# Denominators by block transposes, fewer transfers and a replanned order in an attention and gated-MLP kernel

## The chip, the cores and the metric

The kernel runs on one core of one Trainium2 chip. A core has five engines that run their own instruction streams in order: TensorE (matmul, "PE"), VectorE ("DVE"), ScalarE ("ACT"), GpSimd ("POOL") and SyncE ("SP"), which here issues nearly all transfers between memory (DRAM) and the on-chip buffer. The transfers themselves run on 16 DMA engines. Matmul results go to PSUM, which has eight banks; the kernel uses three as a shared pool (`bs`), two for the large products (`bz`) and three for the outputs (`po`). The metric is device time in microseconds, the median of several runs.

## The reference

Four batches, four heads, 1088 positions, head dimension 32. First a linear attention with a quadratic feature map, whose output x (1088 x 128 per batch) feeds a gated MLP that mixes over positions with a 1088 x 1088 weight matrix.

```python
phi(x) = outer(S1 @ x, S2 @ x)                 # 8 x 8 = 64 features per head and position
kv  = einsum('bhsf,bhsd->bhfd', phi(k), v)
z   = sum(phi(k), over positions)
num = einsum('bhsf,bhfd->bhsd', phi(q), kv)
den = einsum('bhsf,bhf->bhs', phi(q), z) + 1e-06
x   = num / den                                # heads side by side: 128 columns

h    = gelu_tanh(x @ w_in)                     # 1024 columns
u, v = h[..., :512], h[..., 512:]
v_n  = layernorm(v) * g_ln
v_s  = einsum('ts,bsd->btd', w_sg, v_n) + b_sg
out  = x + (u * v_s) @ w_out
```

## The kernel before

Everything is float32; the accurate products are made of three matmuls on a high and a low part (`_h`, `_l`). Columns of positions are cut in three chunks of 362 or 364 (`CH`, `CA`), and the 512 gate columns in four blocks of 128.

The first 50 us are the head: batch 0's attention, the first loads and splits, ordered by a table (`HEAD`). All behind it is built as a list of tasks with an engine, an estimated duration, what they read and write, and buffers they take and free (`Plan.add`). `Plan.order` (L113) then simulates the engines: at each step it issues the task that can begin first, and among equals the one with the earliest due time. Due times come from the TensorE tasks, sorted by `pos`, and are carried back through the dependencies. The result is a fixed order of instructions on each engine.

For each later batch `attention(b)` (L1000) makes x. It loads k and v, makes the key features (L1014 to L1028: `bs`, `kb`, `kp`) and kv with its two parts (`kvh`, `kvl`). Then, for each of three chunks of positions: load q (`qld`, L1039), two parts, project (L1045 to L1047) to 64 rows, copy to `ab` (L1050), store to DRAM as `dq` (L1051), and load back spread out into four tiles e0 to e3 of 128 rows. Of these, two are broadcasts of one transfer each (L1053), and two are written by `spread` (L790 to L793) in eight transfers of 16 rows each. VectorE multiplies them (L1060), ScalarE and VectorE make the two parts (L1061 into `r`, L1062 into `e`), TensorE multiplies by kv (L1069 to L1071). ScalarE copies the result into two tiles: r2 holds the denominators, each repeated over the 32 rows of its head, and r3 the numerators (L1075, L1076).

The denominators then go through DRAM (`dd`): one row of each head out (L1079), back packed into at most 112 rows of 13 (L1080), epsilon and reciprocal (L1081), out (L1082), and back as a broadcast over 32 rows (L1083) into r4. VectorE multiplies r3 by r4 (L1084), and `x_h` and `x_l` are written (L1086, L1087).

From x come the gate's v columns (L1101 to L1103), gelu and its sums (L1110, L1113), the norm (L296 to L332) and the normalised v in `vn` (L340).

`pair(b, p, ...)` (L1130) makes two 128-column blocks of the position mixing with fewer products than plain blocks would take: it uses sums and differences of blocks of the weights. These combinations are made once by `combine` (L961) in eight rounds: load two pieces of the raw weights into `tmp` (L973), combine and split them on VectorE and ScalarE (L978 to L988), store to the DRAM tensors `td` (L991; in the trace `t`, and `tb` for the saved original, L963). Since they don't fit on chip, `stream` (L994) loads the current combination over columns 362 to 723 of `w_h` and `w_l` between products (L996), 24 times in all, four times a pair of transfers. `unit` makes u, `evac` and `gate` bring a product out of PSUM and multiply (`gt`, `gh`, `gl`: L859, L872 to L874), and `gate` ends in the output matmuls (L881 to L883); `store` adds x and stores the output.

In the planner's costs a transfer on SP takes its size over 330 KB per us, at least 0.08 us; `spread` with its eight issues is one task of 200 KB, and a transfer is done 2.0 us after that. `SIDE` gives, per batch, a first due time and a step for the attention's matmuls; output matmuls are due `DELAY` behind their place in the main order.

Of the kernel before, what the change touches and what calls it, by code (L numbers as in the profile page):

```python
# [9 lines left out]
F32 = mybir.dt.float32  # L10
# [24 lines left out]
DELAY = 5.83  # L35
SIDE = [
    dict(k=(0, 0.0241), q=(0.065, 0.0107), n=(0.0314, 0.1822), v=(0.6703, 0.0732)),
    dict(k=(0.0669, 0.0251), q=(0, 0.0934), n=(0.0321, 0.1642), v=(0.3581, 0.0424)),
    dict(k=(0.1528, 0.0085), q=(0, 0.142), n=(0, 0.2213), v=(0.4732, 0.0276)),
]  # L40
START = dict(PE=51.0, V=50.5, A=49.5, G=42.0, SP=22.0)
# [37 lines left out]
class Plan:  # L79
# [9 lines left out]
    def add(self, eng, dur, f, r=(), w=(), take=(), free=(), pos=None, late=None, start=None, after=()):  # L89
# [15 lines left out]
        late = self.LATE.get(eng, 0) if late is None else late  # L105
        self.tasks.append(dict(eng=eng, dur=dur, f=f, deps=deps, take=take, free=list(free), pos=pos, late=late, start=start))
# [6 lines left out]
    def order(self, free, t0):  # L113
# [21 lines left out]
        clock = dict(free)  # L135
        can = {e: [] for e in clock}

# [8 lines left out]
        def enter(i):  # L146
            if T[i]["eng"] is None:
                done(i, T[i]["start"])
            else:
                can[T[i]["eng"]].append(i)  # L150

# [3 lines left out]
        while len(seq) < sum(t["eng"] is not None for t in T):  # L155
            best = None
            for e, c in can.items():
                for i in c:
                    x = max(clock[e], ready[i])
                    for k in T[i]["take"].values():  # L160
                        if not units[k]:
                            break
                        x = max(x, min(units[k])[0])
                    else:
                        key = (x, last[i], i)
                        if best is None or key < best[0]:
                            best = key, i, e
            if best is None:
                raise RuntimeError("stuck: " + str([(T[i]["take"], i) for c in can.values() for i in c][:20]) + str({k: [g for g in self.got if cls[g] == k][-8:] for k in units}))
            (x, _, _), i, e = best  # L170
# [20 lines left out]
def tile_kernel(ctx: ExitStack, tc: tile.TileContext, qd, kd, vd, sd, wd, bd, wind, gd, woutd, identd, outd):  # L191
# [60 lines left out]
    rt, et = ([swap.tile([P, 3 * P], F32, tag=f"{x}{i}", name=f"{x}{i}") for i in range(n)] for x, n in (("r", 5), ("e", 4)))  # L252
# [7 lines left out]
    drt = [const([P, 13], f"dr{i}") for i in range(2)]  # L260
# [504 lines left out]
    t4a = []  # L765
# [586 lines left out]
```

## Time and profile before

| | us |
|---|---|
| median of 3 runs | 434.6 |
| lowest and highest | 433.58, 434.79 |
| the profiled execution | 435.59 |
| its span, first to last instruction | 433.8 |
| its mean granted TensorE clock | 0.921 |

The profile is of one execution. A row of the timeline gives the start, the duration, the engine, the line, the operation with output and inputs, and in brackets the idle time before it and what ended that. SPq is SP's queue of issues. In the chain, which follows the work that ended last backwards, "DMA a<-b" is a transfer from its issue to its landing. A group's row ends in its busy time, the mean duration in ns and the idle time before it. Windows give busy time per engine in a stretch, with the granted clock (1.00 is full speed).

### The profile page before, as it was taken

To read this page: it belongs to the slowest core of one execution; us is meant where nothing else is said; L and a number is where in the kernel's file an instruction comes from. 1 tells how busy PE (TensorE), PEld (TensorE's weight loads), DVE (VectorE), ACT (ScalarE), POOL (GpSimd) and SP (SyncE) were. 2 spreads that over 40 slices of the span, in tenths; PEclk is the share of its full clock that TensorE was granted. 3 is DMA by queue.
4 is the path that set the end of the run, shared out by engine and by line. 5 is a ranking of instruction groups with operands and counts; after the bars stand their busy time and mean duration, and the time that the engine had idled before them with its cause. 6 is when DMAs were issued, how large, how long until landed. Compare 5 with 4: busy or idle time off the path is not lost.

```text
span 433.8 us, 6285 instructions
## 1 busy us (share of the span) xinstructions
PE 365.0 (84%) x1952; PEld 335.1 (77%) x1952; DVE 265.2 (61%) x619; ACT 216.4 (50%) x517; POOL 22.7 (5%) x85
## 2 busy tenths in 40 slices
PE   8989968939487687786968997996876999999996
PEld 7866668939486567686857997996765899899995
DVE  5788957825654483783663545883635565877553
ACT  4667622613234694661363796442422878544320
POOL 0010000000000050000000112000000022100000
PEclk9999997979699998896958999899698899999999
DMA  8990034634476473567663894065844584296351
GB/s 270 402 322 20 0 75 135 178 90 109 112 165 190 102 233 103 165 178 224 161 190 89 240 324 139 13 200 136 231 108 120 155 275 137 71 306 227 103 172 51
DMA packets 63077, 70.72 MB, mean 163 GB/s; under 512 B 10720, under 2 KB 60356, under 8 KB 63044
## 3 DMA queue, kind: packets, MB, share of 16 engines
q1 hardware_dynamic: 62900, 70.24, 54.8%
q8 instruction: 15, 0.25, 0.2%
q14 instruction: 18, 0.15, 0.1%
q10 hardware_dynamic: 144, 0.09, 0.1%
HBM read 61.20 MB, written 9.10 MB: 162 GB/s over the span
## 4 chain that ended last, share of the span: by engine, by line
PE 31%; DMA 24%; SPq 16%; DVE 12%; ACT 9%; issue 5%; POOL 3%; DVEq 0%; POOLq 0%; ACTq 0%
SPq L792 12%; DMA r<-dd 7%; PE bz L927 5%; PE bz L929 5%; PE bz L928 5%; DMA tmp<-in_w 4%; DMA dq<-ab 3%; DMA dd<-dr 3%; ACT vn L340 2%; DMA w_h<-t 2%; ACT kp L1113 2%; PE pz L725 2%; PE pab L601 2%; ACT vn L1110 2%; SPq L1053 1%
## 5 line engine op out<-in xcount | busy, mean ns | idle before, releaser
L927 PE MATMUL bz<-w_h,ar 128*128 128x362 f32 (+1 forms) x288 | 100.5, 349 | 6.0 <-DMA w_h<-t 3.8
L928 PE MATMUL bz<-w_h,ar 128*128 128x362 f32 (+1 forms) x288 | 98.8, 343 | 0.4 <-DVE ar L905 0.4
L929 PE MATMUL bz<-w_l,ar 128*128 128x362 f32 (+1 forms) x288 | 98.8, 343 | 0.0
L927 PEld LDWEIGHTS bz<-w_h,ar 128*128 128x128 f32 x288 | 58.4, 203 | 8.0 <-DMA w_h<-t 4.3
L928 PEld LDWEIGHTS bz<-w_h,ar 128*128 128x128 f32 x288 | 58.0, 201 | 1.4 <-DVE ar L905 0.6
L929 PEld LDWEIGHTS bz<-w_l,ar 128*128 128x128 f32 x288 | 57.6, 200 | 0.2 <-DMA w_l<-t 0.2
L1060 DVE TENSOR_TENSOR e<-e,e 128x364 f32<-128x364 f32 (+1 forms) x18 | 9.6, 536 | 45.6 <-DMA e<-dq 38.4
L1061 ACT CAST r<-e 128x364 fp32r<-128x364 f32 (+1 forms) x18 | 8.9, 494 | 55.0 <-DVE e L1060 54.9
L874 DVE TENSOR_TENSOR gl<-gt,gh 128x362 fp32r<-128x362 f32 (+1 forms) x47 | 25.1, 533 | 17.3 <-ACT gh L873 17.2
L873 ACT CAST gh<-gt 128x362 fp32r<-128x362 f32 (+1 forms) x47 | 23.2, 493 | 23.9 <-DVE gt L872 22.9
L340 ACT ACTIVATE vn<-vn,st 128x512 f32<-128x512 f32 x36 | 27.9, 811 | 9.9 <-POOL st L332 5.8
L904 ACT CAST ar<-vn 128x512 fp32r<-128x512 f32 x40 | 24.7, 617 | 13.3 <-PE bz L929 12.9
L905 DVE TENSOR_TENSOR ar<-vn,ar 128x512 fp32r<-128x512 f32 x40 | 27.4, 684 | 3.8 <-ACT ar L904 3.4
L849 ACT ACTIVATE u<-bs 128x362 f32<-128x362 f32 (+1 forms) x48 | 22.3, 468 | 12.8 <-PE bs L845 11.4
L883 PE MATMUL po<-gl,wout_h 128*128 128x362 f32 (+1 forms) x47 | 16.7, 354 | 12.7 <-DVE gl L874 12.7
L872 DVE TENSOR_TENSOR gt<-gt,u 128x362 f32<-128x362 f32 (+1 forms) x47 | 25.0, 532 | 1.5 <-ACT u L849 0.9
L859 DVE SCALAR_TENSOR_TENSOR gt<-bz,g_col,b_bc 128x362 f32<-128x362 f32 (+1 forms) x31 | 18.3, 591 | 9.3 <-PE bz L939 5.1
L1101 PE MATMUL bs<-win_h,x_h 128*128 128x512 f32 x27 | 12.7, 471 | 11.2 <-ACT x_h L1086 4.8
L843 PE MATMUL bs<-x_h,win_h 128*128 128x362 f32 (+1 forms) x48 | 16.6, 345 | 6.5 <-ACT r L1076 3.8
L1084 DVE TENSOR_TENSOR r<-r,r 128x364 f32<-128x364 f32 (+1 forms) x9 | 4.8, 537 | 26.9 <-DMA r<-dd 26.9
L883 PEld LDWEIGHTS po<-gl,wout_h 128*128 128x128 f32 x47 | 9.3, 199 | 13.7 <-DVE gl L874 13.6
L1022 PE MATMUL bs<-vx,kp 128*128 128x128 f32 x108 | 19.1, 310 | 0.8 <-DVE kp L268 0.8
(267 smaller groups left out, 803.2 us busy)
## 6 DMA issues: line engine op xcount, KB each, us to landing
w_h<-t SPq DMA_DIRECT2D x72, 181.0 KB
w_l<-t SPq DMA_DIRECT2D x72, 181.0 KB
w_f<-in_w SPq DMA_DIRECT2D x9, 544.0 KB
t<-tmp SPq DMA_DIRECT2D x48, 90.5 KB
w_h<-tb SPq DMA_DIRECT2D x24, 181.0 KB
w_l<-tb SPq DMA_DIRECT2D x24, 181.0 KB
tmp<-in_w SPq DMA_DIRECT2D x16, 181.0 KB
vx<-in_v SPq DMA_DIRECT2D x8, 288.0 KB
```

Source lines behind the costliest of these rows:

```text
L340: A.activation(self.vn(t), self.vn(t), AF.Identity, bias=self.nm[:, t : t + 1], scale=self.rs[:, t : t + 1])
L792: last = load(e[16 * i : 16 * i + 16], d)
L849: add("A", 0.05 + ac(cw), lambda: A.activation(utt[plan.got[u]][:, :cw], ps(k)[:, :cw], AF.Gelu_apprx_tanh), r=[k], take={u: "u"}, free=[k])
L872: add("V", dv(cw), lambda: V.tensor_mul(gt(k)[:, :cw], gt(k)[:, :cw], utt[plan.got[u]][:, :cw]), r=[u], w=[k], free=[u])
L873: add("A", ac(cw), lambda: A.copy(ght[plan.got[h]][:, :cw], gt(k)[:, :cw]), r=[k], take={h: "gh"})
L874: add("V", dv(cw), lambda: V.tensor_sub(glt[plan.got[l]][:, :cw], gt(k)[:, :cw], f32(ght[plan.got[h]][:, :cw])), r=[h, k], take={l: "gl"}, ...
L883: mm(o, lhsT=wout_h[:, db], rhs=hl, start=False, stop=i == NB, skip_group_check=True)
L904: add("A", ac(n), lambda: A.copy(dst[:, 0], q()), r=r, w=[key])
L905: add("V", dv(n), lambda: V.tensor_sub(dst[:, 1], q(), f32(dst[:, 0])), r=r, w=[key])
L927: mm(o, lhsT=ar[e][:, 0, t], rhs=wh, start=first, stop=False, skip_group_check=True)
L928: mm(o, lhsT=ar[e][:, 1, t], rhs=wh, start=False, stop=False, skip_group_check=True)
L929: mm(o, lhsT=ar[e][:, 0, t], rhs=wl, start=False, stop=last, skip_group_check=True)
```

## The change

It has three parts.

The denominators stay on chip. r2 holds each denominator on all 32 rows of its head, so a transpose of its 32 x 32 blocks on VectorE leaves in every 32nd column of r4 the denominators of 32 positions, one in each row. Epsilon and reciprocal act on 12 columns; ScalarE spreads each over 32 columns of r2, and a second transpose brings them to the layout of the numerators. The columns of r2 behind the shortest chunk are set to one once.

Transfers are merged. The four spread tiles become two tiles of two halves, ea and eb; each half of eb is loaded by one transfer whose source repeats 16 rows eight times, and product, cast and subtraction act on both halves at once. `combine` stores three combinations' parts by three transfers instead of six, and the saved original by five instead of eight. `stream` loads two slices of `w_h` by one transfer; `w_l` stays at one each. The keys of the dependencies are kept apart for the two parts.

The planner counts 0.47 us of SP for each issue (1.0 for the two of ea or eb), and a transfer's end by a ring that moves 300 KB per us. `SIDE` becomes a table with a due time for each attention matmul group, `UNITS` and `OUTS` give offsets of the unit and output matmuls, and `STARTS` the batches' starts. The search for the next task is also rewritten, with the same rule.

```diff
-DELAY = 5.83
+START = dict(PE=51.0, V=50.5, A=49.5, G=42.0, SP=22.0)
+STARTS = (0.0, 96.0, 166.0, 236.0)
 SIDE = [
-    dict(k=(0, 0.0241), q=(0.065, 0.0107), n=(0.0314, 0.1822), v=(0.6703, 0.0732)),
-    dict(k=(0.0669, 0.0251), q=(0, 0.0934), n=(0.0321, 0.1642), v=(0.3581, 0.0424)),
...
+        k=[-69.5, -129.7, -258.62, 75.49, -16.81, -86.04, 99.22, -240.4, 467.74],
+        m=[44.69, -2.17, -319.74, 128.68, -11.47, -380.37, -268.7, -327.69, -223.35],
+        q=[-500.43, 26.57, 6.61],
+        n=[-114.19, -31.31, 54.44, 107.92, 21.3, 18.55],
+        v=[79.56, 57.62, 53.21, 95.41, 35.99, 315.99, 135.47, 134.1, 132.66],
...
+UNITS = [
+    [-875.2, 12.55, 557.21],
...
+OUTS = [
+    [12.14, 10.35, 36.95],
...
-        late = self.LATE.get(eng, 0) if late is None else late
+        late = (2.3 + kb / 300 if eng == "SP" else self.LATE.get(eng, 0)) if late is None else late
...
+            if e == "SP":
+                ring = max(ring, clock[e]) + T[i]["kb"] / 300
+                T[i]["late"] = max(2.1, ring + 1.7 - clock[e])
...
-    dma = lambda kb: max(0.08, kb / 330.0)
+
+    def load_(_, kb, f, **kw):
+        return add("SP", 0.47, f, kb=kb, **kw)
...
     def combine():
+        load_("td", 740, lambda: load(td[3, :, 0].rearrange(by), f32(w_h[:, 4:8, 362:724])), r=[("w", t + 4, 1, 0) for t in range(4)], w=[("td", "b", t, 0) for t in range(4)])
         for t in range(4):
-            add("SP", dma(370), lambda t=t: [load(td["b"][t, 0], f32(w_h[:, t + 4, 362:724])), load(td["b"][t, 1], f32(w_l[t + 4][:, 362:724]))],
-                r=[("w", t + 4, 1)], w=[("td", "b", t)])
...
-                for n, i, j in (("1", 0, 0), ("3", 1, 1), ("2", 3, 2)):
-                    add("SP", dma(186), lambda t=t, c=c, s=s, hi=hi, n=n, i=i, j=j: [
-                        load(td[n][t, 0][:, c : c + HW], f32(hi[:, j])), load(td[n][t, 1][:, c : c + HW], s[:, i])],
-                        r=[k[i], hk[j]], w=[("td", n, t)])
+                nk = [("td", n, t, i) for i in range(2) for n in "132"]
+                load_("td", 278, lambda t=t, c=c, hi=hi: load(td[:3, t, 0, :, c : c + HW].rearrange(by), f32(hi)), r=hk, w=nk[:3])
+                load_("td", 186, lambda t=t, c=c, s=s: load(td[:2, t, 1, :, c : c + HW].rearrange(by), s[:, :2]), r=k[:2], w=nk[3:5])
+                load_("td", 93, lambda t=t, c=c, s=s: load(td[2, t, 1, :, c : c + HW], s[:, 3]), r=[k[3]], w=nk[5:])
 
     def stream(n, half):
         for t in range(4):
-            add("SP", dma(370), lambda t=t: [load(f32(w_h[:, t + half, 362:724]), td[n][t, 0]), load(f32(w_l[t + half][:, 362:724]), td[n][t, 1])],
-                r=[("td", n, t)], w=[("w", t + half, 1)])
+            if t % 2 == 0:
+                load_("w", 371, lambda t=t: load(f32(w_h[:, half + t : half + t + 2, 362:724]), TD[n][t : t + 2, 0].rearrange(by)),
+                    r=[("td", n, x, 0) for x in (t, t + 1)], w=[("w", half + x, 1, 0) for x in (t, t + 1)])
+            load_("w", 186, lambda t=t: load(f32(w_l[half + t][:, 362:724]), TD[n][t, 1]), r=[("td", n, t, 1)], w=[("w", half + t, 1, 1)])
...
-            add("SP", dma(93), lambda cw=cw, ci=ci: load(dq[ci][:, :cw], abt[:, :cw]), r=["ab"], w=[("dq", ci)])
-            for p in range(2):
-                add("SP", dma(200), lambda cw=cw, ci=ci, p=p: load(
-                    here(f"e{p}")[:, :cw], dq[ci][16 * p : 16 * p + 16, :cw].unsqueeze(1).broadcast_to([16, R, cw])),
-                    r=[("dq", ci)], w=[("e", p)])
-                add("SP", dma(200), lambda cw=cw, ci=ci, p=p: spread(
-                    here(f"e{2 + p}")[:, :cw], dq[ci][32 + 16 * p : 48 + 16 * p, :cw]),
-                    r=[("dq", ci)], w=[("e", 2 + p)])
-            for p in range(2):
-                add("V", dv(cw), lambda p=p, cw=cw: V.tensor_mul(now[f"e{p}"][:, :cw], now[f"e{p}"][:, :cw], now[f"e{2 + p}"][:, :cw]), r=[("e", 2 + p)], w=[("e", p)])
-                add("A", ac(cw), lambda p=p, cw=cw: A.copy(here(f"r{p}", F32R)[:, :cw], now[f"e{p}"][:, :cw]), r=[("e", p)], w=[("r", p)])
-                add("V", dv(cw), lambda p=p, cw=cw: V.tensor_sub(here(f"e{2 + p}", F32R)[:, :cw], now[f"e{p}"][:, :cw], f32(now[f"r{p}"][:, :cw])), r=[("e", p), ("r", p)], w=[("e", 2 + p)])
+            load_("", 93, lambda cw=cw, ci=ci: load(dq[ci][:, :cw], abt[:, :cw]), r=["ab"], w=[("dq", ci)])
+            for i, e in enumerate(("ea", "eb")):
+                def fill(cw=cw, ci=ci, i=i, e=e):
+                    d = dq[ci][32 * i : 32 * i + 32, :cw].rearrange("(p x) c -> x p c", p=2)
+                    o = here(e)[:, :, :cw]
+                    if i:
+                        for p in range(2):
+                            load(o[:, p], dq[ci][32 + 16 * p : 48 + 16 * p, :cw].unsqueeze(0).broadcast_to([R, 16, cw]))
+                    else:
+                        for p in range(2):
+                            load(o[:, p], dq[ci][16 * p : 16 * p + 16, :cw].unsqueeze(1).broadcast_to([16, R, cw]))
+
+                add("SP", 1.0, fill, kb=373, r=[("dq", ci)], w=[e])
+            add("V", dv(2 * cw), lambda cw=cw: V.tensor_mul(now["ea"][:, :, :cw], now["ea"][:, :, :cw], now["eb"][:, :, :cw]), r=["eb"], w=["ea"])
+            add("A", ac(2 * cw), lambda cw=cw: A.copy(here("r0", F32R)[:, :, :cw], now["ea"][:, :, :cw]), r=["ea"], w=["r0"])
+            add("V", dv(2 * cw), lambda cw=cw: V.tensor_sub(here("eb", F32R)[:, :, :cw], now["ea"][:, :, :cw], f32(now["r0"][:, :, :cw])), r=["ea", "r0"], w=["eb"])
...
-            n = CD[ci]
-            dr = drt[0][: H * (cw // n), :n]
-            add("SP", 0.08, lambda cw=cw, ci=ci: load(dd[ci][0, :, :cw], now["r2"][0:P:32, :cw]), r=[("r", 2, 0), ("r", 2, 1)], w=[("dd", ci)])
-            add("SP", 0.08, lambda cw=cw, ci=ci, n=n, dr=dr: load(dr, dd[ci][0, :, :cw].rearrange("h (i n) -> h i n", n=n)), r=[("dd", ci)], w=["dr"])
-            add("V", 0.5, lambda dr=dr: [V.tensor_scalar(dr, dr, EPS, None, op0=ALU.add), V.reciprocal(dr, dr)], w=["dr"])
-            add("SP", 0.08, lambda cw=cw, ci=ci, n=n, dr=dr: load(dd[ci][1, :, :cw].rearrange("h (i n) -> h i n", n=n), dr), r=["dr"], w=[("dd", ci)])
-            add("SP", dma(190), lambda cw=cw, ci=ci: load(now["r4"][:, :cw], dd[ci][1, :, :cw].unsqueeze(1).broadcast_to([H, 32, cw])), r=[("dd", ci)], w=[("r", 4)])
-            add("V", dv(cw), lambda cw=cw: V.tensor_mul(now["r3"][:, :cw], now["r3"][:, :cw], now["r4"][:, :cw]), r=[("r", 4)], w=[("r", 3, 0), ("r", 3, 1)])
+            add("V", dv(3 * P), lambda: V.transpose(now["r4"], now["r2"]), r=[("r", 2, 0), ("r", 2, 1)], w=["r4"])
+
+            def invert():
+                V.tensor_scalar(drt, now["r4"][:, : 3 * P : 32], EPS, None, op0=ALU.add)
+                V.reciprocal(drt, drt)
+
+            add("V", 0.4, invert, r=["r4"], w=["dr"])
+            add("A", ac(3 * P), lambda: A.copy(now["r2"].rearrange("p (n i) -> p n i", i=32), drt.unsqueeze(2).broadcast_to([P, 12, 32])), r=["dr"], w=[("r", 2, 0), ("r", 2, 1)])
+            add("V", dv(3 * P), lambda: V.transpose(now["r4"], now["r2"]), r=[("r", 2, 0), ("r", 2, 1)], w=["r4"])
+            add("V", dv(cw), lambda cw=cw: V.tensor_mul(now["r3"][:, :cw], now["r3"][:, :cw], now["r4"][:, :cw]), r=["r4"], w=[("r", 3, 0), ("r", 3, 1)])
...
-    starts, LONG = [0.0], (104.0 - 8, 70.0, 70.0, 58.0)
...
+    add("G", 0.1, lambda: G.memset(now["r2"][:, 360:], 1.0), w=[("r", 2, 0), ("r", 2, 1)])
```

More of the change, by code (lines that the diff above doesn't have):

```diff
@@ L87, in __init__, with add @@
         self.wrote, self.read = {}, {}
-    def add(self, eng, dur, f, r=(), w=(), take=(), free=(), pos=None, late=None, start=None, after=()):
+    def add(self, eng, dur, f, r=(), w=(), take=(), free=(), pos=None, late=None, start=None, after=(), kb=0):
         n = len(self.tasks)
@@ L134, in order @@
         self.got, seq = {}, []
-        clock = dict(free)
+        clock, ring = dict(free), 0.0
         can = {e: [] for e in clock}
+        stale = set(can)
+        users_of = {c: {t["eng"] for t in T if c in t["take"].values()} for c in self.units}
         def done(i, at):
@@ L154, in order @@
                 enter(i)
[L155 to L158, printed above, removed]
+        total = sum(t["eng"] is not None for t in T)
+        best = {}
+        while len(seq) < total:
+            for e in stale:
+                best[e] = None
+                for i in can[e]:
                     x = max(clock[e], ready[i])
@@ L259, in tile_kernel @@
     stats = [const([P, 4 * NT + 40], f"st{i}") for i in range(2)]
-    drt = [const([P, 13], f"dr{i}") for i in range(2)]
+    drt = const([P, 12], "dr")
     for i in range(WARM):
@@ L781, in tile_kernel, with here @@
     pe = lambda n: 0.005 + n * 0.443e-3
-    dma = lambda kb: max(0.08, kb / 330.0)
+    def load_(_, kb, f, **kw):
+        return add("SP", 0.47, f, kb=kb, **kw)
     now = {}
-    def here(tag, dt=F32, k=None):
-        now[k or tag] = swap.tile([P, 3 * P], dt, tag=tag, name=tag)
-        return now[k or tag]
-    def spread(e, d):
-        for i in range(R):
-            last = load(e[16 * i : 16 * i + 16], d)
-        return last
+    def here(tag, dt=F32):
+        now[tag] = swap.tile([P, 3 * P] if tag > "r0" else [P, 2, 3 * P], dt, tag=tag, name=tag)
+        return now[tag]
     for i in (2, 3, 4):
@@ L820, in tile_kernel, with pemain @@
     for t in range(NT):
-        lo = add("V", 1.29, head.s.steps["wlo", t][2], w=[("w", t, c) for c in range(3)], after=[lo] if t else [])
+        lo = add("V", 1.29, head.s.steps["wlo", t][2], w=[("w", t, c, 1) for c in range(3)], after=[lo] if t else [])
     done_lo = lo
     clock = [0.0]
-    def pemain(dur, f, d=0.0, **kw):
+    def pemain(dur, f, d=0.0, main=True, **kw):
         i = add("PE", dur, f, pos=clock[0] + d, **kw)
-        if d == 0.0:
+        if main:
             clock[0] += dur
```

153 lines of the change are left out of this document (104 added, 49 removed).

## The prediction

> **What bounds the kernel now.** I read the page's span, busy shares and chain first, then busy time by stage, then the timelines of TensorE, VectorE and the SP queue around the places where TensorE stands.
>
> ```profile
> span 433.8 us, 6285 instructions
> PE 31%; DMA 24%; SPq 16%; DVE 12%; ACT 9%; issue 5%; POOL 3%; DVEq 0%; POOLq 0%; ACTq 0%
> ```
>
> Transfers and the SP queue (SPq, the engine that issues nearly all transfers) hold 40% of the chain that ended last, TensorE 31%. Busy time by stage shows where. I cut the span behind the head where a batch's pairs begin (about 170, 262 and 372 us). Columns: busy us of PE, PEld, DVE, ACT and POOL with instructions, granted clock, DMA share, GB/s.
>
> ```profile
> 60.00:170.00 110.00, 79.83 (x416) 73.82 (x415) 61.60 (x151) 50.18 (x139) 7.12 (x23) 0.88 0.51 138
> 170.00:262.00 92.00, 77.81 (x395) 73.63 (x395) 52.37 (x115) 51.85 (x125) 3.46 (x12) 0.87 0.68 197
> 262.00:372.00 110.00, 93.85 (x513) 88.80 (x513) 64.29 (x140) 56.83 (x140) 9.32 (x33) 0.92 0.52 146
> 372.00:434.00 62.00, 57.02 (x335) 55.31 (x334) 39.30 (x76) 21.22 (x43) 0.00 (x0) 0.99 0.50 159
> 400.00:420.00 20.00, 20.00 (x122) 20.00 (x121) 10.81 (x19) 6.27 (x12) 0.00 (x0) 1.00 0.49 149
> ```
>
> From 400 to 420 us TensorE runs undisturbed: 122 matmuls in 20 us, 0.164 us each. At that pace the first three stages' 416, 395 and 513 matmuls would take 68, 65 and 84 us, 217 in all; they took 312. The **95 us lost** split in two. TensorE stood for 30.2 + 14.2 + 16.2 = 60.5 us (length less busy). And the granted clock was 0.88, 0.87 and 0.92: 0.12 x 110 + 0.13 x 92 + 0.08 x 110 = 34 us. The fourth stage, whose weights stream just as much but which has no attention beside it, lost 62 - 55 = 7. So it is the attention work of the next batch, and the weight combining in the first stage, that holds TensorE up. The timelines say how:
>
> ```profile
> 66.91 0.79 PE L1014 MATMUL bs<-sk,vn 128*128 128x128 f32 x2 [5.28 <-DVE kp L268]
> 95.82 0.67 PE L883 MATMUL po<-gl,wout_h 128*128 128x364 f32 x1 [6.89 <-DVE gl L874]
> 114.28 0.67 PE L883 MATMUL po<-gl,wout_h 128*128 128x362 f32 x1 [5.77 <-DVE gl L874]
> 199.64 0.67 PE L927 MATMUL bz<-w_h,ar 128*128 128x362 f32 x1 [3.80 <-DMA w_h<-t]
> 305.82 0.67 PE L1071 MATMUL bs<-e,kvh 128*128 128x364 f32 x1 [3.92 <-DVE e L1062]
> ```
> ```profile
> 92.60 0.54 DVE L1060 TENSOR_TENSOR e<-e,e 128x364 f32<-128x364 f32 x1 [5.92 <-DMA e<-dq]
> 94.97 0.35 DVE L978 TENSOR_TENSOR tmp<-tmp 128x181 f32<-128x181 f32 x1 [1.83 <-DMA tmp<-in_w]
> 95.23 0.53 DVE L874 TENSOR_TENSOR gl<-gt,gh 128x364 fp32r<-128x364 f32 x1
> ```
> ```profile
> 87.54 3.62 SPq L792 DMA_DIRECT2D e<-dq  x8
> 91.20 0.49 SPq L1051 DMA_DIRECT2D dq<-ab  x1
> 91.73 0.58 SPq L1080 DMA_DIRECT2D dr<-dd  x1
> 92.36 0.95 SPq L973 DMA_DIRECT2D tmp<-in_w  x2
> ```
>
> Read the 6.89 us backwards. TensorE waits for gl, which VectorE makes at 95.23. VectorE runs in order and stood first 5.92 us for e, then 1.83 us for tmp; gl needed neither. Both loads were late because SP was issuing a run of eight small transfers (L792). The other four gaps have the same root, and after each TensorE pays again in clock:
>
> ```profile
> 96.49 0.30 PE bz L927
> 100.39 0.17 PE bz L927
> ```
>
> These rows of the chain are the same matmul just behind the 6.89 us gap and 4 us later.
>
> **The change, part by part.** *Spread.* Per chunk the kernel issues e in 18 transfers, 2 broadcasts (L1053) and 16 small ones (L792); after, 4. Two issues of SP's timeline (start, us), then two transfers of the chain:
>
> ```profile
> 55.62 0.56 SPq L1053 DMA_DIRECT2D e<-dq  x1
> 60.67 3.82 SPq L792 DMA_DIRECT2D e<-dq  x8
> 64.08 1.72 DMA e<-dq
> 92.36 2.58 DMA tmp<-in_w
> ```
>
> From 55.62 to the landing at 65.80 (64.08 + 1.72) is 10.2 us. After: 4 issues at the 0.56 us of L1053 are 2.2 us, plus a landing. A load of 181 KB of ordinary shape (tmp<-in_w) landed 2.58 us after issue, so 4.8 us at best. But the new eb load repeats 16 rows eight times with the repeat outermost, and the one load in the trace with a small repeat outermost (r<-dd, 4 heads) is slow: its 5.41 us is quoted with the round trip below. With that, 2.2 + 5.4 = 7.6 us. Bounds 4.8 and 7.6; I take 7, near the row of like shape. The Trainium skill, "DMA: Bandwidth & Descriptors", "Rules for kernel authors", speaks against this edit: a leading zero-stride broadcast of c copies confines a transfer to at most c of the 16 engines, so eb would use 8. By it both halves put 45 KB on each engine, as r<-dd does on 4, and 7.6 us would be the value instead of 7. The trace agrees as far as that 5.41 us goes.
>
> *Fewer transfers.* Counts of issues that shrink:
>
> ```profile
> w_h<-t SPq DMA_DIRECT2D x72, 181.0 KB
> w_h<-tb SPq DMA_DIRECT2D x24, 181.0 KB
> t<-tmp SPq DMA_DIRECT2D x48, 90.5 KB
> e<-dq SPq DMA_DIRECT2D x96, 22.8 KB
> e<-dq SPq DMA_DIRECT2D x48, 22.5 KB
> ```
>
> Stream reloads fall from 192 (72 + 24, and as many for w_l) to 144, stores of combined weights from 48 to 24, of tb from 8 to 5, e from 162 (18 broadcasts, 144 small) to 36, denominators from 36 to 0: 237 issues less. A run of eight takes 3.8 us, 0.47 each, so SP is freed of about 111 us. I give that no term of its own: it is worth what it takes off TensorE's gaps. Bytes stay nearly the same. Cost: two w_h slices now come as one transfer of twice the size, issued when the second is free and waited for whole (and SP, waiting for that, holds back dq and e behind it). Its 181 KB more take 0.9 us at the 197 GB/s of the second stage's row: between 0 (SP early) and 0.9 us on each of 48 such loads, 44 in all. I take 3, near the lower end, because the fourth stage streams at 0.50 DMA share with TensorE full.
>
> *Denominators.* Before, a trip out and back by four transfers, of which the chain has the first and the last:
>
> ```profile
> 229.20 4.42 DMA dd<-r
> ...
> 238.42 5.41 DMA r<-dd
> 243.86 0.55 DVE r L1084
> ```
>
> 14.7 us from issue to product. After: transpose, add and reciprocal, a ScalarE spread, transpose. Nearest rows:
>
> ```profile
> L673 DVE TENSOR_TENSOR x_l<-px,x_h 128x384 fp32r<-128x384 f32 x3 | 1.6, 543 | 0.0
> L739 DVE TENSOR_TENSOR w_l<-w_f,w_h 128x1088 fp32r<-128x1088 f32 (+1 forms) x9 | 11.6, 1285 | 0.0
> L1081 DVE RECIPROCAL dr<-dr 112x13 f32<-112x13 f32 (+1 forms) x9 | 2.1, 236 | 0.3
> L669 ACT CAST x_h<-px 128x384 fp32r<-128x384 f32 x3 | 1.4, 476 | 0.1
> ```
>
> No transpose is in the trace: at least the 0.24 us of the short reciprocal, at most the 1.29 us of 1088 columns; I take 0.54, same columns. Chain: 0.54 + 0.24 (the add, taken as the reciprocal) + 0.24 + 0.48 + 0.54 = 2.0 us (1.4 to 3.5), with hand-overs say 2.5: 12 us shorter in each of nine chunks. The new waits are for ScalarE (the copies of q3's result, then the spread), and behind them in VectorE's order stand kp, gl and the evacuations that TensorE waits for; waits of about half a microsecond take the place of the one for r. VectorE does 18 x 0.54 = 9.7 us more (4.3 to 23). The merged product and subtraction on 728 columns are 0.91 us each, between the rows of 384 and 1088, for two of 0.53 (gl's row, 364 columns): 18 x 0.15 = 2.7 back. But in series product, cast and subtraction now wait for all of e: 3 x 0.38 = 1.1 us later in each chunk, out of the 12 won. It is 0.56 to 0.58 busy in the three stages, so this lies beside other work; were the stages 15% shorter it would be near 0.7. If that cover fails, the 7 us fall on the path. The Trainium skill, "VectorE: DVE Perf Modes", "The three transpose paths", gives 311 ns for 128x128 bf16; three of those, an estimate, are 0.93 us, and the chain would be 0.8 us longer in each chunk; no run shows it yet. One memset on GpSimd, 3 to 9 us busy in these stages, and the last batch's sums in other tiles cost nothing.
>
> *The order.* Each issue now counts as 0.47 us and a transfer holds the ring by its size; before, a run of eight counted as 0.61 (200/330) against 3.8 measured. So the old order put loads behind SP that it believed free. Every unit, output and attention matmul gets its own due time; what that does alone no row shows. Its ends: it wins no more than the standing that is left, and loses no more than the slower rival below; I put nothing on it beyond the terms here.
>
> **The sum.** The five quoted gaps are 25.7 us; three quarters go (e lands a third sooner, and SP, with half the issues, issues it without a queue): -19.3. Two more gaps stand behind r<-dd:
>
> ```profile
> 149.25 0.49 PE L1101 MATMUL bs<-win_h,x_h 128*128 128x512 f32 x1 [3.15 <-ACT x_h L1086]
> 337.26 0.43 PE L843 MATMUL bs<-x_h,win_h 128*128 128x362 f32 x1 [3.81 <-ACT r L1076]
> ```
>
> They go: -7.0. The other 27.8 us of standing are small gaps of mixed origin; I take -8. New waits +3. Standing -31.3. Clock follows standing: 34 x 31.3 / 60.5 = -17.6. Together -49, a span of 385. The profiled execution took 435.59 us, 1.8 beyond its span; the median of the runs is 434.6, 0.8 beyond it: **386 us**, 11% faster, own range 373 to 399.
>
> **Rivals.**
> 1. *TensorE becomes the bound.* All named gaps go and 20 of the 27.8: -52.7, clock -29.6, **352 us**. For it: the fourth stage shows TensorE can run so. Against it: the second stage's DMA share is 0.68 x 92 = 63 us of engine time, against 65 of TensorE work, so transfers would have to fit almost perfectly.
> 2. *VectorE still stands for e.* eb lands as r<-dd did, and its four waits in order remain: half of the named gaps (-12.9), half of those behind r<-dd, as x is late because e is late (-3.5), new waits +3, clock -7.5: -21, **414 us**. For it, the 5.41 us row; against it, SP's freed time lets e be asked for earlier.
> 3. *The issues were hidden anyway.* Gaps move to other waits of the same length: **434 us**. Against it: SP is at work without a break before the quoted gap.
> 4. *Reloads late: slower.* w_h now comes in pairs behind one wait. If the new order leaves TensorE standing at each of 24 streams as it did once at 199.64 (3.80 us), that is 91 us against 49 won. It decides from 49 / 24 = 2.0 us per stream; with 2.5 us it is 60 - 49 = +11, **446 us**. Against it: reloads in the fourth stage cost no gap.
>
> **How the numbers follow.** Forecast 0.50, rival 1 0.20, rival 2 0.22, rival 3 0.02, rival 4 0.06. A time within 0.3% (1.3 us) can't be told from no change. Faster is the first three, 0.92; same 0.02; slower 0.06. The range takes the forecast and the greater part of rivals 1 and 2, each with a few us about its number: 350 to 418.
>
> **What would show it.** Right: SP's share of the chain falls from 16% to a few per cent; VectorE's standing for e is well under the present; no wait for dd; x follows the last q3 by 5 us or so; pairs begin near 140, 222 and 312 us instead of 170, 262 and 372; clock 0.95 or more. Wrong: VectorE waits for eb as long as before (rival 2), TensorE waits for w_h<-td at many streams (rival 4), a transpose well over 1.3 us, or gaps behind ScalarE, whose part I left unchanged.

## The result and the profile after

| | us, median | lowest and highest | ratio to before, 95% interval |
|---|---|---|---|
| before | 434.27 | 433.58, 434.79 | |
| after | 348.19 | 347.09, 349.42 | 0.802, 0.798 to 0.806 |
| forecast | 386 | 350 to 418 | |

The kernel is 86 us faster. The direction was forecast, the size was not: the time lies just below the range, next to rival 1 (TensorE becomes the bound, 352 us). The page of after, its span and its chain of waits:

```profile
span 345.3 us, 5940 instructions
PE 70%; DMA 13%; DVE 11%; issue 2%; ACT 2%; SPq 1%; DVEq 0%
```

SP's queue, 16% of the chain before, is 1%; TensorE went from 31% to 70%. Busy time by stage, with the columns of the prediction's table, cut at 133, 208 and 283 us, 2 to 15 us behind the first step of a batch's pairs on VectorE (131, 199 and 268; cut there, the standing below comes to the same 5.4 us):

```profile
60.00:133.00 73.00, 69.75 (x423) 66.56 (x422) 63.61 (x154) 53.00 (x143) 7.20 (x23) 1.00 0.63 184
133.00:208.00 75.00, 73.26 (x444) 70.87 (x443) 60.76 (x132) 55.83 (x140) 6.44 (x22) 1.00 0.84 251
208.00:283.00 75.00, 74.59 (x439) 73.02 (x438) 58.38 (x122) 53.02 (x125) 6.37 (x22) 1.00 0.59 186
283.00:346.00 63.00, 58.36 (x348) 57.55 (x347) 39.20 (x75) 19.66 (x39) 0.00 (x0) 0.97 0.49 160
```

Length less busy: TensorE stands 3.25 + 1.74 + 0.41 = 5.4 us in the three stages, where it stood 60.5 before, and the clock is full. So 55 us of standing are gone, and the 34 us that the low clock cost went with them: 89 us, and the span fell by 433.8 - 345.3 = 88.5. TensorE's busy time says the same of the clock: behind the head it is 308.5 us in the prediction's four rows and 276.0 in these, 32.5 less. In the second stage the transfers hold 0.84 x 75 = 63 us of engine time, the same 63 as before (0.68 x 92) in a shorter stage.

The order of VectorE's waits changed with it. Before (engine, line, what it waited for: us in total, times, longest):

```profile
DVE e L1060 <- DMA e<-dq: 38.4, 13, 5.9
DVE r L1084 <- DMA r<-dd: 26.9, 8, 6.3
DVE tmp L978 <- DMA tmp<-in_w: 16.9, 5, 8.6
```

After, the rows of the same view for these loads and for ScalarE's new step, below the two longest waits that VectorE now has:

```profile
DVE ar L968 <- ACT ar L967: 13.7, 10, 3.7
DVE gt L922 <- PE bz L1004: 13.3, 13, 3.3
DVE ea L1133 <- DMA eb<-dq: 5.5, 4, 2.1
DVE tmp L1045 <- DMA tmp<-in_w: 1.5, 3, 0.8
DVE r L1150 <- ACT r L1148: 1.0, 2, 0.6
DVE r L1158 <- ACT r L1157: 0.6, 1, 0.6
```

82 us of standing behind three kinds of loads became 7, and the two new waits for ScalarE are 1.0 and 0.6 us. VectorE now stands longest for ScalarE's part of `ar` and for TensorE's results. The two longest gaps left on TensorE behind the head, from its timeline:

```profile
122.23 0.71 PE L1091 MATMUL bs<-vx,kp 128*128 128x128 f32 x4 [1.72 <-DVE kp L335]
156.19 0.43 PE L992 MATMUL bz<-w_h,ar 128*128 128x362 f32 x1 [1.26 <-DMA w_h<-td]
```

Nothing of 3 to 7 us is left. Only the second stands behind a pair of reloads (`w_h`), which is what rival 4 feared.

### The profile page after: what moved, and what is told of

It is laid out like the page before. It is cut to its first block, busy times and chain, and to the rows that moved or that the text cites. A ratio compares the mean times of both kernels' runs of the same rounds, so it can differ in the third digit from the quotient of the medians.

```text
span 345.3 us, 5940 instructions
## 1 busy us (share of the span) xinstructions
PE 332.4 (96%) x1952; PEld 311.4 (90%) x1952; DVE 271.4 (79%) x619; ACT 217.7 (63%) x517; POOL 23.0 (7%) x86
## 4 chain that ended last, share of the span: by engine, by line
PE 70%; DMA 13%; DVE 11%; issue 2%; ACT 2%; SPq 1%; DVEq 0%
PE bz L992 12%; PE bz L993 11%; PE bz L994 11%; DMA eb<-dq 4%; DMA td<-tmp 3%; PE pz L792 3%; PE bs L1091 2%; PE pab L668 2%; DMA tmp<-in_w 2%; DMA w_h<-td 2%; PE bs L906 2%; PE bs L907 2%; PE bs L908 2%; PE bz L1004 2%; PE bz L1003 2%
## 5 line engine op out<-in xcount | busy, mean ns | idle before, releaser
L992 PE MATMUL bz<-w_h,ar 128*128 128x362 f32 (+1 forms) x288 | 95.6, 332 | 1.9 <-DMA w_h<-td 1.3
L993 PE MATMUL bz<-w_h,ar 128*128 128x362 f32 (+1 forms) x288 | 94.7, 329 | 0.2 <-DVE ar L968 0.2
L994 PE MATMUL bz<-w_l,ar 128*128 128x362 f32 (+1 forms) x288 | 94.7, 329 | 0.0
L992 PEld LDWEIGHTS bz<-w_h,ar 128*128 128x128 f32 x288 | 54.3, 188 | 3.7 <-DMA w_h<-td 1.7
L993 PEld LDWEIGHTS bz<-w_h,ar 128*128 128x128 f32 x288 | 54.2, 188 | 1.0 <-DVE ar L968 0.5
L994 PEld LDWEIGHTS bz<-w_l,ar 128*128 128x128 f32 x288 | 54.2, 188 | 0.0
L936 ACT CAST gh<-gt 128x362 fp32r<-128x362 f32 (+1 forms) x47 | 23.1, 496 | 21.7 <-DVE gt L935 10.9
L1188 ACT ACTIVATE kp<-vn,st 128x512 bf16<-128x512 f32 x27 | 19.5, 721 | 0.2
L1091 PE MATMUL bs<-vx,kp 128*128 128x128 f32 x108 | 16.4, 276 | 1.7 <-DVE kp L335 1.7
L792 PE MATMUL pz<-w_f,vn 128*128 128x362 f32 (+3 forms) x54 | 17.6, 472 | 0.3 <-ACT vn L407 0.3
L1185 ACT ACTIVATE vn<-bs 128x512 f32<-128x512 f32 x27 | 15.9, 590 | 1.7 <-PE bs L1178 1.7
L1091 PEld LDWEIGHTS bs<-vx,kp 128*128 128x128 f32 x108 | 14.6, 191 | 2.0 <-DVE kp L335 2.0
L907 PE MATMUL bs<-x_h,win_l 128*128 128x362 f32 (+1 forms) x48 | 15.7, 328 | 0.0
```

What stands on the lines that cost most here:

```text
L792: return mm(zs[ci], lhsT=vn[r, t, :P], rhs=w_f[t][r, c0 : c0 + cw], start=(t == 0), stop=(t == NT - 1),)
L936: add("A", ac(cw), lambda: A.copy(ght[plan.got[h]][:, :cw], gt(k)[:, :cw]), r=[k], take={h: "gh"})
L992: mm(o, lhsT=ar[e][:, 0, t], rhs=wh, start=first, stop=False, skip_group_check=True)
L993: mm(o, lhsT=ar[e][:, 1, t], rhs=wh, start=False, stop=False, skip_group_check=True)
L994: mm(o, lhsT=ar[e][:, 0, t], rhs=wl, start=False, stop=last, skip_group_check=True)
L1091: mm(ps(pkv)[:, P * p : P * p + P], lhsT=kpt[t % 3][:, P * p : P * p + P], rhs=vx[:, NT : NT + t + 2 : t + 1] if p else vx[:, t : NT + 1 : ...
```

## The experiments

Fourteen kernels, each compared with runs of the kernel before on the same chip; those medians lay between 434.9 and 435.5 us. With the few runs that each had, an interval reaches 2 to 7 us to either side, so differences under 8 us between two of them are read with care.

### The order apart from the instructions

Three kernels keep all of after's instructions (and its rewritten search) and take the planning of before, in parts. e1 takes the old due times, e2 the old costs, e3 both.

```diff
 e1
-UNITS = [
...
+UNITS = [[0.0] * 3 for _ in range(16)]
+OUTS = [[DELAY] * 3 for _ in range(16)]
 e2
-        late = (2.3 + kb / 300 if eng == "SP" else self.LATE.get(eng, 0)) if late is None else late
+        late = self.LATE.get(eng, 0) if late is None else late
...
-                ring = max(ring, clock[e]) + T[i]["kb"] / 300
-                T[i]["late"] = max(2.1, ring + 1.7 - clock[e])
...
-        return add("SP", 0.47, f, kb=kb, **kw)
+        return add("SP", max(0.08, kb / 330.0), f, kb=kb, **kw)
...
```

In e1 `SIDE` is also filled from the old starts and steps.

> The changed kernel with its transfers, transposes and planner costs, but with the due times of before: first time and step per batch for the attention's matmuls, outputs 5.83 us behind, units without offsets. Theory T (SP's freed issues and the removed round trip carry the gain, any sensible order uses them): 350 to 370 us, TensorE standing under 20 us behind the head. Theory O (the due-time tables carry it; without them the side chain is late again): 385 us or more, with gaps of 2 us and longer behind kp, gl or x_h.

> The changed kernel with its due-time tables, but the planner counts a transfer as before: size over 330 KB per us on SP, at least 0.08 us, done 2.0 us later, no ring. With the merged transfers these costs are not far from 0.47 us per issue, so if dearer issues matter only through the spread, which is gone, this stays at 348 to 358 us. If the ring and the issue price are what times the loads (theory C), loads come too late or SP is over-booked again: 370 us or more.

> The changed kernel's instructions with both the due times and the transfer costs of before: the first two parts of the change alone. Theory T: 355 to 375 us. Theory O or C: 390 us or more. The difference to 348 is what the replanned order is worth; the difference to 434 what the instructions are worth.

Measured: e1 359.3 us (ratio 0.826, 0.811 to 0.842), e2 360.1 (0.828, 0.814 to 0.843), e3 367.5 (0.845, 0.832 to 0.858). So the instructions with the planning of before give 68 us of the 86, and the new planning 19 on top: without its due times 11 us are lost (e1), without its costs 12 (e2). e1 and e3 lie where theory T put them, e2 between its two cases. Behind 60 us e3 looks like this:

```profile
60.00:367.20 307.20, 285.06 (x1660) 275.59 (x1659) 223.76 (x483) 184.22 (x445) 19.03 (x67) 0.98 0.61 184
```

Behind the head TensorE stands 307.2 - 285.1 = 22 us, in after 9 (285.3 less the four busy times above), and in before 65.5, by the prediction's four rows (374 less 308.5). The forecast of -49, which by its own words held nothing for the order, is to be held against e3's -68.

### The parts of the change alone

e4 puts only the transposes into the kernel before; e5 only the merged tiles ea and eb with their 4 loads for 18; e6 is e3 with the denominators sent through DRAM again, so all merges without the transposes.

```diff
 e4
-            add("SP", 0.08, lambda cw=cw, ci=ci: load(dd[ci][0, :, :cw], now["r2"][0:P:32, :cw]), r=[("r", 2, 0), ("r", 2, 1)], w=[("dd", ci)])
...
+            add("V", dv(3 * P), lambda: V.transpose(now["r4"], now["r2"]), r=[("r", 2, 0), ("r", 2, 1)], w=[("r", 4)])
...
 e5
-                add("SP", dma(200), lambda cw=cw, ci=ci, p=p: spread(
-                    here(f"e{2 + p}")[:, :cw], dq[ci][32 + 16 * p : 48 + 16 * p, :cw]),
...
+                            load(o[:, p], dq[ci][32 + 16 * p : 48 + 16 * p, :cw].unsqueeze(0).broadcast_to([R, 16, cw]))
...
+                add("SP", 1.2, fill, r=[("dq", ci)], w=[e])
```

> The kernel before with the denominators transposed on VectorE, all else of before (spread, single reloads, costs, due times). By my sum the round trip is worth 7.0 us of standing and 3.9 of clock: 423 us. If SP's order (it waits in line at dd for earlier steps of the trip) is worth more than the trip itself, 400 to 415 us. If e's lateness sets x anyway: 430 to 434 us.

> The kernel before with only ea and eb: four loads in place of 18 per chunk, and product, cast and subtraction on both halves; round trip, single reloads, costs and due times of before. 126 SP issues less (59 us of SP's time). Together with the transposes (412.8) the remaining merges must make up for what the three parts give in the old plan (367.5). Theory S (SP's issues for e are the root of the quoted gaps): 385 to 400 us, VectorE's standing for e down from 38 us to under 20. Theory L (what counts is the length of the side chain, of which e's load is only 3 us shorter and the merged arithmetic 1 us longer): 415 us or more.

> The changed kernel's merged transfers with the denominators through DRAM as before, and costs and due times of before. If the parts add up, 434 - (435 - 367.5) + 22 = 390 us. If the round trip is what is late once SP is free (it is 14.7 us long whatever SP does), 395 to 410 us, with TensorE's gaps behind x_h. If with SP free the trip is hidden beside the stages, 368 to 378 us.

Measured: e4 412.8 us (0.949, 0.937 to 0.961), e5 391.9 (0.902, 0.895 to 0.910), e6 384.9 (0.886, 0.875 to 0.897). From before by e5, e6 and e3 to after: -43, -7, -17, -19. The -7 of the other merges is at the edge of what these runs tell. e4 lies in its second case; e5's time lies where theory S put it, but VectorE's standing for e is 24.4 us there and not under 20; e6 lies between its cases. In e5 VectorE's waits are

```profile
DVE ea L1061 <- DMA eb<-dq: 24.4, 9, 4.1
DVE r L1085 <- DMA r<-dd: 18.5, 8, 4.4
```

Both fell from before (38.4 and 26.9), although nothing was done about dd. SP, free of the small issues, may reach dd's transfers sooner; but the order was made anew too, and the two weren't parted.

### What the small issues cost

e7 is after in exactly its own order, with each half of eb loaded by eight issues of 16 rows (126 issues more). e8 is after in its own order with each paired reload of `w_h` split again into two transfers (48 issues more).

```diff
 e7
-                            load(o[:, p], dq[ci][32 + 16 * p : 48 + 16 * p, :cw].unsqueeze(0).broadcast_to([R, 16, cw]))
+                            for r in range(R):
+                                load(o[16 * r : 16 * r + 16, p], dq[ci][32 + 16 * p : 48 + 16 * p, :cw])
 e8
-                load_("w", 371, lambda t=t: load(f32(w_h[:, half + t : half + t + 2, 362:724]), TD[n][t : t + 2, 0].rearrange(by)),
+                load_("w", 371, lambda t=t: [load(f32(w_h[:, half + x, 362:724]), TD[n][x, 0]) for x in (t, t + 1)],
```

> The changed kernel with the very same order on every engine; only each half of eb is loaded by eight issues of 16 rows. 126 issues and 59 us of SP's time come back. Theory S: SP is late again behind each run of 16, 370 to 390 us. Theory L or O: under 355 us, since SP has spare time in this kernel.

> The changed kernel with the very same order; only w_h is reloaded by one transfer per slice, 48 issues more (23 us of SP's time over 300 us). If issues count wherever they stand: 353 to 360 us. If only the runs in front of the side chain's loads count: within 2 us of 348. A slice that no longer waits for its neighbour's bytes could also win 1 or 2 us.

Measured: e7 389.2 us (0.896, 0.886 to 0.906), 41 more than after; e8 347.9 (0.801, 0.792 to 0.810), the same as after within the 4 us of its interval. The chain of e7 and VectorE's longest wait there:

```profile
PE 57%; DMA 14%; SPq 14%; DVE 7%; ACT 3%; issue 3%; DVEq 0%; POOL 0%; ACTq 0%; POOLq 0%
DVE ea L1134 <- DMA eb<-dq: 35.1, 8, 5.9
```

SP's queue and the wait for e are nearly back at before's 16% and 38.4 us. It looks like the price of 126 issues, 0.33 us each. It is no fixed price, as e9 shows: in e7 the order still is the one that was planned for four issues.

### Are the small issues dear, or only unknown to the planner?

e9 is the kernel before with every instruction kept and only the planner's costs set to what its own trace shows. e13 adds the merged e loads to that, e14 instead adds the transposes.

```diff
-    dma = lambda kb: max(0.08, kb / 330.0)
+    dma = lambda kb: max(0.47, kb / 330.0)
...
-                add("SP", dma(200), lambda cw=cw, ci=ci, p=p: spread(
+                add("SP", 3.8, lambda cw=cw, ci=ci, p=p: spread(
...
-            add("SP", 0.08, lambda cw=cw, ci=ci: load(dd[ci][0, :, :cw], now["r2"][0:P:32, :cw]), r=[("r", 2, 0), ("r", 2, 1)], w=[("dd", ci)])
+            add("SP", 0.47, lambda cw=cw, ci=ci: load(dd[ci][0, :, :cw], now["r2"][0:P:32, :cw]), r=[("r", 2, 0), ("r", 2, 1)], w=[("dd", ci)])
...
```

> The kernel before with every instruction as it was; only the planner's costs are set to what the trace of before shows: a transfer issue takes at least 0.47 us of SP, a run of eight 3.8 us. Its order is made anew from these. Theory A, that SP's time itself is short: the 126 small issues cost SP the same time in any order, so this gains little: 425 to 440 us. Theory B, that the old planner merely put loads behind an SP that it believed free: with true costs it places them well, and most of what the e merge gave alone (43 us) comes without it: 390 to 405 us.

> The kernel before with the e loads merged (4 transfers a chunk for 18) and with at least 0.47 us of SP for each issue in the plan; denominators through DRAM, all else of before. True costs alone gave 401, the merge alone 392. Theory A, that the merge's 43 us are SP's time itself and the costs a second, separate gain: about 360 to 372 us. Theory B, that both cure the same thing, SP's runs of eight standing in front of loads at the wrong place: 380 to 392 us.

> The kernel before with the denominators transposed on VectorE and with the true costs of SP's issues in the plan (0.47 us each, a run of eight 3.8 us); e still by 18 transfers a chunk. The transposes alone gave -22 us, true costs alone -34. Theory A, that the way through DRAM is a wait of its own: they add up, 375 to 385 us. Theory B, that its four issues only suffered from SP's queue: 392 to 401 us.

Measured: e9 401.4 us (0.921, 0.917 to 0.925), e13 391.4 (0.900, 0.894 to 0.906), e14 368.8 (0.848, 0.838 to 0.858). Theory B of e9 holds: numbers in the planner alone, with the 162 loads of e as they were, give 34 us. Theory B of e13 holds: the merge and the true costs cure the same thing, 43 and 34 apart and 43.5 together. Theory A of e14 holds, and by more than it said (368.8 for 375 to 385): with true costs the transposes give 33 us where alone they gave 22. VectorE's waits in e9, and its wait for e in e13:

```profile
DVE r L1084 <- DMA r<-dd: 27.2, 9, 6.7
DVE e L1060 <- DMA e<-dq: 7.9, 3, 3.5
```
```profile
DVE ea L1061 <- DMA eb<-dq: 19.8, 6, 4.4
```

The wait for e fell from 38.4 to 7.9 us with the same 18 transfers a chunk; the wait for dd stayed at 27. In e13, with 4 transfers and the true costs, VectorE stands longer for e than in e9. So the two cures don't remove the same waits one by one, and that e13's order is merely a poorer one isn't excluded. VectorE's timeline in before, then in e9, says how:

```profile
61.49 0.54 DVE L1060 TENSOR_TENSOR e<-e,e 128x364 f32<-128x364 f32 x1 [2.13 <-DMA e<-dq]
65.98 0.54 DVE L1060 TENSOR_TENSOR e<-e,e 128x364 f32<-128x364 f32 x1 [3.95 <-DMA e<-dq]
```
```profile
65.77 0.54 DVE L1060 TENSOR_TENSOR e<-e,e 128x364 f32<-128x364 f32 x1 [0.34 <-issue]
66.49 0.54 DVE L1060 TENSOR_TENSOR e<-e,e 128x364 f32<-128x364 f32 x1 [0.18 <-DMA qld<-in_q]
```

The chunk's second product comes at nearly the same moment, 66.5 for 66.0 us, and SP's last issue of this chunk's e ends at 63.4 us for 64.5 (62.21 + 1.22 in e9, 60.67 + 3.82 in before), so e is had hardly sooner. But VectorE has other work until then, where before the products were put ahead of it and VectorE stood 2.1 and 3.9 us in front of them. The wait for dd didn't yield to the costs; why the planner found nothing to put in front of it was not tried. TensorE's busy time and granted clock behind the head, in e9 and then e14:

```profile
60.00:400.30 340.30, 297.21 (x1647) 275.64 (x1646) 216.88 (x481) 179.97 (x442) 19.24 (x67) 0.94 0.62 175
```
```profile
60.00:368.60 308.60, 287.09 (x1649) 275.41 (x1648) 225.74 (x500) 184.27 (x452) 18.27 (x67) 0.96 0.62 187
```

TensorE stands 43 us in e9 and 21.5 in e14, against 65.5 in before.

Set side by side, one way from before to after goes by true costs (e9, -34), transposes (e14, -33), the merges with the ring in the plan (e1, -10) and the due times (after, -11). The intervals of e14 and e1 overlap a little, the others don't. Each of these kernels has an order of its own, so each step also holds what that order happens to be worth. How far the time moves when the planner's costs are changed without any meaning was not run; it bears most on the steps of about 10 us.

### What bounds the kernel now

e11 issues each of the 18 transposes twice with the same operands. e12 leaves out the third matmul of each of the 48 products of u. e10 moves the repeat of eb's load inwards, by which x is computed from rows in another arrangement and the output is another. All three keep after's order.

```diff
 e11
-            add("V", dv(3 * P), lambda: V.transpose(now["r4"], now["r2"]), r=[("r", 2, 0), ("r", 2, 1)], w=["r4"])
+            add("V", dv(3 * P), lambda: [V.transpose(now["r4"], now["r2"]), V.transpose(now["r4"], now["r2"])], r=[("r", 2, 0), ("r", 2, 1)], w=["r4"])
 e12
-            mm(o, lhsT=win_h[:, ws], rhs=xl[:, cs], start=False, stop=True)
 e10
-                            load(o[:, p], dq[ci][32 + 16 * p : 48 + 16 * p, :cw].unsqueeze(0).broadcast_to([R, 16, cw]))
+                            load(o[:, p], dq[ci][32 + 16 * p : 48 + 16 * p, :cw].unsqueeze(1).broadcast_to([16, R, cw]))
```

> The kernel after in the same order; each of the 18 transposes is issued twice in a row with the same operands, which changes no value. VectorE gets 18 x 0.57 = 10.3 us more, and each chunk's way from q3 to x is 1.1 us longer. Theory A, that TensorE bounds and VectorE's work lies beside it: 348 to 351 us. Theory B, that the cover is thin (VectorE is busy 0.87, 0.81 and 0.78 of the stages): 352 to 360 us, the 10.3 us falling on the path in whole or nearly so.

> The kernel after in the same order; each of the 48 products of u leaves out its third matmul (w_in's high part by x's low part), so u is less exact. TensorE has 48 matmuls less at 0.164 us each, 7.9 us. Theory A, that TensorE bounds (rival 1 of the prediction): the time falls by about as much, to 339 to 342 us. Theory B, that something beside TensorE now sets the pace and TensorE only just keeps up: 345 us or more.

> The kernel after in the same order; in the load of eb the repeat is moved inwards (16 source rows, each repeated eight times, as in ea), so eb holds its rows in another arrangement and x is another. Same bytes, same count of issues. By the Trainium skill (DMA: Bandwidth & Descriptors, Rules for kernel authors) the repeat of eight outermost confines eb to 8 of 16 engines, so here eb should land markedly sooner than in after, where the chain has it at 3.1 to 5.3 us. Theory A: the time stays at 348 us within 1%, as TensorE stands for only 5 us behind the head. Theory B: eb's landing still holds up VectorE enough to count: 343 us or less.

Measured: e11 352.2 us (0.811, 0.807 to 0.815), e12 343.9 (0.789, 0.786 to 0.793), e10 344.8 (0.792, 0.789 to 0.795). Against after's 0.798 to 0.806 all three differ. e11's time lies among theory B's, but 10.3 us more on VectorE cost 4 and not nearly all. e10 lies at the lower edge of theory A, 1.0% under after. e12 lies between its theories: it gave 4 us by the medians and 5.6 by the ratios, and its 48 matmuls less took 5.3 us off TensorE's busy time, not the 7.9 that were expected. The page's line of TensorE, after and then e12:

```profile
PE 332.4 (96%) x1952; PEld 311.4 (90%) x1952; DVE 271.4 (79%) x619; ACT 217.7 (63%) x517; POOL 23.0 (7%) x86
```
```profile
PE 327.1 (95%) x1904; PEld 303.9 (89%) x1904; DVE 270.8 (79%) x619; ACT 217.0 (63%) x517; POOL 23.0 (7%) x86
```

Its idle time is 345.3 - 332.4 = 12.9 us in after and 342.7 - 327.1 = 15.6 in e12. But each is one execution, after's the shortest of its four (spans 345.3 to 347.6) and e12's one of its longer ones (340.1 to 343.4), so whether the relief came back whole or turned in part into waiting can't be told from them. TensorE sets most of the pace; that e11 and e10 move the time too shows that what feeds it is only just fast enough.

e10 gave 3.4 us by the medians and 4.5 by the ratios. VectorE's wait for eb in e10:

```profile
DVE ea L1133 <- DMA eb<-dq: 2.6, 1, 2.6
```

Half of after's 5.5. The DMA share shows why. In after the 16 engines are busy for 0.48 of the stretch from 58.00 to 59.75 us, in which only rows of eb move; in e10 they are busy for 0.93 from 57.75 to 58.50, again with rows of e alone, and the last of them is through at 59.2 us for 60.9. This agrees with the rule of the Trainium skill that the prediction weighed ("DMA: Bandwidth & Descriptors", "Rules for kernel authors": an outermost repeat of eight keeps a transfer on at most 8 of 16 engines): 0.48 of 16 engines are nearly 8. In before the row that the prediction took for it, r<-dd, whose outermost dimension is the four heads, holds 0.26 from 239.70 to 240.30 us, which is 4. After's chain has three landings of eb,

```profile
75.61 4.48 DMA eb<-dq
87.36 3.08 DMA eb<-dq
115.55 5.25 DMA eb<-dq
```

and in e10 the view of the tile gives

```profile
DMA to landing us min/median/max: 2.8/3.8/7.5
```

The chain shows the landings that were waited for, not all of them, so these two views can't be set against each other. A version with the right arrangement and the repeat inside was not run: it would have to write every sixteenth partition by one transfer.

## Why the prediction was wrong, by its own steps

**What bounds the kernel: right in the amount, wrong in one cause.** 95 us were put down to standing and clock, and 89 came back. But of the 6.89 us gap it was said that both loads were late "because SP was issuing a run of eight small transfers". e9 keeps the runs of eight, and VectorE's standing for e falls to 7.9 us. For e, the loads were late *in the order that the planner had made*; SP's time as such was the lesser part (10 us, e13 against e9).

**The order: the step that failed.** "So the old order put loads behind SP that it believed free" was stated and then priced at nothing ("I put nothing on it beyond the terms here"). True costs alone gave 34 us (e9), due times a further 11 (after against e1). In the forecast's own terms, as an addition to the new instructions, the order was worth 19 (after against e3): half of the 38 us between forecast and result. The other half is the next step.

**The gaps were counted too narrowly.** With the planning of before the new instructions gave 68 us (e3), not 49. Of the standing, the forecast took off 31.3; e3 took off 65.5 - 22.1 = 43, and after 55 in the three stages. "The other 27.8 us of standing are small gaps of mixed origin; I take -8" was mis-sized: at most 5.4 us of any standing is left there in after, so at least 22 of the 27.8 went. They were not all small, and most of them were not of another origin. Two of them in TensorE's timeline of before:

```profile
167.18 0.67 PE L843 MATMUL bs<-x_h,win_h 128*128 128x364 f32 x1 [2.70 <-DVE kp L268]
219.06 0.79 PE L1101 MATMUL bs<-win_h,x_h 128*128 128x512 f32 x1 [3.14 <-ACT r L1076]
```

Of the 27.4 us that this timeline lists beside the seven counted gaps, 18.8 name kp, e with its cast, r or x_h: the same steps of the next batch's attention that four of the seven name. That the same cure reached them is what e3 and after show together; no run takes them gap by gap. The clock followed: 34 x 55.1 / 60.5 = 31 by the forecast's rule, and all 34 came back (32.5 by TensorE's busy time).

**Spread.** e in 7 us, bounds 4.8 and 7.6. SP's timeline of after and VectorE's:

```profile
54.79 1.22 SPq L1130 DMA_DIRECT2D ea<-dq  x2
56.06 1.31 SPq L1127 DMA_DIRECT2D eb<-dq  x2
73.71 1.20 SPq L1130 DMA_DIRECT2D ea<-dq  x2
113.65 1.20 SPq L1130 DMA_DIRECT2D ea<-dq  x2
```
```profile
61.59 0.91 DVE L1133 TENSOR_TENSOR ea<-ea,eb 128x728 f32<-128x728 f32 x1
```

From 54.79 to the product's start are 6.8 us, and that product didn't wait, so e was in by then. For the chunks issued from 73.71 and 113.65 us the landing is on the chain quoted above, at 80.09 and 120.80: 6.4 and 7.2 us. The duration was right, the four issues 2.5 us for 2.2. The row behind the upper bound was misread: r<-dd repeats inside (32 rows to each head), and what it shares with eb's load is only the short outermost dimension.

**Denominators.** The durations were right. Rows of the tile r (min, median and max in ns):

```profile
L1150 DVE STREAM_TRANSPOSE r<-r x9: 569/572/579, 84.3 to 234.2; 128x384 f32<-128x384 f32 x9
L1153 DVE TENSOR_SCALAR dr<-r x9: 159/171/175, 85.2 to 235.1; 128x12 f32<-128x12 f32 x9
L1157 ACT COPY r<-dr x9: 504/511/514, 86.1 to 236.1; 128x384 f32<-128x384 f32 x9
```

0.572 us against 0.54 taken, 0.51 for the spread against 0.48. The estimate of 0.93 from the Trainium skill's "VectorE: DVE Perf Modes", "The three transpose paths", was too dear; the measurement decides. But the term, the two gaps behind r<-dd (-7.0, and 10.9 with their share of the clock), was half of what the transposes gave alone (22, e4) and a third of what they gave with true costs (33, e14 against e9). VectorE stood 26.9 us for r<-dd in 8 places, and behind it gl, evacuations and `ar` were queued. Even of the gaps of TensorE that name x_h or r, six with 14.1 us, the forecast counted two. The cover for the 7 us of added work on VectorE is thin, as was said: twice the transposes cost 4 of 10.3 us.

x follows later than forecast. The last q3 of the last chunk, on TensorE, and the last product of the way to x, on VectorE:

```profile
232.88 0.33 PE L1144 MATMUL bs<-eb,kvh 128*128 128x360 f32 x1
```
```profile
240.19 0.52 DVE L1162 TENSOR_TENSOR x_l<-r,x_h 128x360 fp32r<-128x360 f32 x1
```

In this chunk it is 7.5 us from the end of the one to the end of the other, where 5 or so were expected: other work on both engines stands between the steps. TensorE didn't wait for it.

**Fewer transfers.** No term of its own was given to 111 us of SP's time, as worth only what it takes off TensorE's gaps. The runs bear that out: the e merge, 126 issues less, gives 43 us under the old costs (e5) and 10 under the true ones (e13 against e9). The 3 us for reloading `w_h` in pairs don't show: e8, without the pairs, is the same as after within 4 us.

**The pairs** were to begin near 140, 222 and 312 us. By VectorE's timeline they begin 9, 23 and 44 us before that:

```profile
131.33 0.68 DVE L1225 TENSOR_TENSOR vn<-vn 128x512 f32<-128x512 f32 x1
199.37 0.69 DVE L1225 TENSOR_TENSOR vn<-vn 128x512 f32<-128x512 f32 x1
267.68 0.68 DVE L1225 TENSOR_TENSOR vn<-vn 128x512 f32<-128x512 f32 x1
```

**Rivals.** Rival 1 happened, at 348 for 352, with a chance of 0.20. What was held against it, that transfers "would have to fit almost perfectly" into the second stage, was read right: 63 us of them lie in its 75, at 0.84. It was no reason against it. TensorE needs 73 us there, and the transfers go on beside it as long as they are asked for early enough, which is what the order does. Rivals 2 to 4 did not happen; rival 3 is right in a part, as the issues could have been hidden anyway by a better order.

## What to carry to other kernels

Where an engine runs in a fixed order, the gap in front of a late load has two cures, a faster load or other work put in front of the wait; before removing transfers, give the planner their measured cost and see what is left. Here the two did not add up for e (34 and 43 us apart, 43.5 together), while the round trip of the denominators cost the same wait under the better costs, and taking it away gave more there (33 us) than under the old ones (22). And when five gaps have one root, count all the standing with that root, the small gaps too, and the clock that returns with it.

## What the runs showed of the hardware that was not expected

Putting back the 126 small issues costs 41 us in an order planned without them (e7 against after). Where the plan knows their cost, the kernel with them takes 10 us more than the one without (e9 against e13, the merged arithmetic included): what an issue on SP costs depends on the order around it. The clock came back whole: 0.91 behind the head in before is the mean of the prediction's rows weighted by time, 0.94 and 0.96 in e9 and e14, 1.00 through 223 us of after in which TensorE stands 5.4 us. A load whose source has its repeat of eight outermost kept the DMA engines 0.48 busy where it ran alone, with the repeat inside 0.93 (after and e10). A transpose of 128x384 in float32 on VectorE took 0.572 us, hardly more than a subtraction of 384 columns (0.543, in the prediction's rows).
